# Tile 0's mean in two halves, tile 2 and tile 3 trade their way of transposing, and projections by quarters of the weights

## The chip, the cores and the metric

The kernel runs on one core of a Trainium2 chip. The metric is the device time of one launch in microseconds (us), the median of several runs. The core has five engines with instruction streams of their own that wait for each other by semaphores: TensorE (PE, matmuls; its weight loads are shown as PEld), VectorE (DVE), ScalarE (ACT), GpSimd (POOL) and SyncE (SP), which issues nearly all DMAs here. Matmuls write to PSUM, which has eight banks of 128 x 512 float32.

## The reference

A layer norm feeds a linear-attention block and a gated feed-forward block; the input and both results are added.

```python
x  = A_x                                   # 1 x 2048 x 512, bfloat16
xn = (x - mean(x)) / sqrt(var(x) + 1e-5)   # over the last axis

# A: linear attention, 32 heads of 16
q, k, v = split(xn @ wqkv)                 # wqkv 512 x 1536
phi = lambda t: where(t > 0, t + 1, exp(t)) + 1e-6
pq, pk = phi(q), phi(k)
kv  = einsum("bhsd,bhse->bhde", pk, v)
z   = einsum("bhsd->bhd", pk)
o   = (pq @ kv) / (pq . z + 1e-6)          # by head
A   = o @ wo                               # wo 512 x 512

# B: feed-forward, width 1792
B   = (silu(xn @ w_gate) * (xn @ w_up)) @ w_down

return x + A + B
```

## The kernel before, in words

The 2048 rows are 16 tiles of 128 rows (t = 0 to 15); a tile's 512 columns are four quarters of 128 (c = 0 to 3). There is no scheduler. The kernel calls small helpers in a hand-written order; each helper appends one operation to one engine's list through `K.op` or `K.dma` and names what it reads and writes, and a recording class (`_Prog`) works out the semaphore waits. An engine runs its list strictly in the order of the calls, so the order of the calls in the code is the order on each engine, and a waiting instruction holds back all that stands behind it on its engine.

The program has three stages.

1. *Start*, lines 593 to 700: tiles 0 to 4, written out by hand. This is where the change lies.
2. *Projection loop*, lines 706 to 735: for tiles 5 to 15, K = xn Wk and Q = xn Wq (`kproj`, `qproj`), the feature map of K, and `gtacc(t)`, which sums xn^T pk over the tiles in banks 4 to 7.
3. *FFN loop*, lines 978 to 1001: the gated feed-forward, the normalisation of Q and the output tiles.

What the start does for a tile, by helper:

- `xload` loads x, `wqkv_load` a part of Wq or Wk by quarters of its rows. They stand ahead of everything (lines 247 to 259). SP issues them one after the other; two go through ScalarE's queue.
- `bns` (bn_stats, line 296) and `agg` (bn_aggr, line 299) give mean and variance on VectorE, `eps` adds 1e-5 (VectorE or POOL), `rstd_of` raises to the power -0.5 on POOL (line 352).
- `mean_act(1)` (line 304) sums tile 1 on ScalarE with an accumulator, so that its mean needs no bn_stats.
- Tiles 0, 1 and 2 are not normalised ahead of their projections: they are only centred (`xc_half`, line 379, half a tile; `xc_full`, line 389, a whole one), and the scale rstd is applied when the projection is read out of PSUM (`first_ek`, `first_pk`, `first_pq`, lines 503 to 525).
- A centred tile is transposed either on TensorE, `tp_first` (two matmuls with the identity, line 407, and a copy to SBUF on ScalarE, line 416), or by a DMA on SP, `transpose_xc` (line 398). Before the change tiles 0 and 1 go through TensorE and tile 2 through the DMA.
- `proj_first(t, name, h)` (line 446) is half of a projection: two matmuls, quarters 2h and 2h+1.
- From tile 3 on, tiles are normalised whole (`xn_dve`, line 332), transposed by DMA into xnT (`transpose_dma`, line 423) and projected with `kproj` and `qproj` (line 432). ScalarE and VectorE make the features with `exp_k`, `exp_q`, `copy_q`, `clip_k` and `maxadd_k`.
- The FFN needs xnT of tiles 0 to 2 as well; their transposes run in the loop (lines 719 and 720), and `late_eq` makes their exponential of Q there (lines 727 and 728).
- `feat_pool(0)` makes tile 0's K feature on POOL, `first_feat` those of tiles 1 and 2 on VectorE. `xn_act(0)` normalises tile 0 on ScalarE, with `negmean(0)` on POOL for its bias.
- `fill(n, cols)` (line 268) issues matmuls on constants, whose result nobody reads, while TensorE has nothing else.

K of tile t uses bank 0 or 2 and Q bank 1 or 3 (even and odd t); the transposes of the start use banks 4 to 7.

## Time and profile before

| | |
|---|---|
| three timed runs | 210.83, 210.95, 211.18 us; median 210.95 |
| the profiled execution, its own time | 210.89 us |
| its span (first to last instruction) | 209.7 us |
| granted TensorE clock, mean | 1.00 |
| busy: TensorE, VectorE, POOL, ScalarE | 206.7, 119.4, 74.4, 70.2 us |
| VectorE busy, 0 to 5, 5 to 10, 10 to 15 us | 2.13, 4.29, 4.54 us |
| ScalarE busy, the same | 2.54, 4.64, 3.30 us |
| POOL busy, the same | 1.79, 3.19, 2.15 us |

Times inside the profile count from the start of the span. A row of the order of time reads: start, length, engine, line, operation, what it writes and reads, shape, how many were merged, and in brackets how long the engine had been idle before it and what ended that. A matmul of 512 columns is shown 0.38 us long, but matmuls overlap, so the next one starts much earlier: the distance of their starts is what they cost. Lists of waits read: who waited, for whom, us in total, how often, the longest.

DMA landings in the profile before, in us: x of tile 0 at 2.78, of tile 1 at 3.18, of tiles 2 to 5 at 5.92, 7.24, 8.42 and 8.74; Wk quarters 0 and 1 at 4.53, 3 at 4.67, 2 at 4.89; Wq quarters 0 to 3 at 6.27, 6.67, 7.67 and 8.09. The load of tiles 6 and 7 (256 KB) is issued at 8.60 and lands at 11.35.

### The profile page before, as it was taken

Reading aid. Unit: us, or ns where it says so; the run is one execution under the profiler, and the core shown is the slowest. Engines: PE = TensorE matmul, PEld = TensorE weight load, DVE = VectorE, ACT = ScalarE, POOL = GpSimd, SP = SyncE. Lnnn points to the kernel's source line nnn. Section 1 sums busy time; section 2 is a strip of 40 time slices with the busy share of each in tenths; the row PEclk is TensorE's granted clock in tenths of the full one; section 3 lists DMA queues with packets and bytes.
Section 4 is the critical chain, followed back from the end, with each engine's and each line's share of the span. In section 5 each row is a group of like instructions: output and inputs, shape, how many; then the busy total and the mean of one; then the engine's idle time right before and its main releaser. Section 6 shows DMA issues by size and latency. Waiting matters only on the chain.

```text
span 209.7 us, 2763 instructions
## 1 busy us (share of the span) xinstructions
PE 206.7 (99%) x983; PEld 94.7 (45%) x983; DVE 119.4 (57%) x243; ACT 70.2 (33%) x123; POOL 74.4 (35%) x96
## 2 busy tenths in 40 slices
PE   8999999999999999999999999999999999999996
PEld 3344444445444444444444444444444444444444
DVE  4899988336265774637355746365556535373222
ACT  5957667956633331302122312213031213121000
POOL 3648987567032443223141422240424132221200
DMA  6766344894791111010202110202021010410201
GB/s 204 196 182 172 69 88 100 276 363 138 218 347 34 22 28 26 27 25 28 50 2 50 25 28 25 50 0 50 4 49 25 27 25 25 49 30 27 50 25 53
DMA packets 30287, 16.84 MB, mean 80 GB/s; under 512 B 20928, under 2 KB 29632, under 8 KB 30272
## 3 DMA queue, kind: packets, MB, share of 16 engines
q1 hardware_dynamic: 29984, 16.39, 29.6%
q10 hardware_dynamic: 288, 0.26, 0.4%
q8 instruction: 8, 0.13, 0.3%
q14 instruction: 7, 0.06, 0.1%
HBM read 9.70 MB, written 2.10 MB: 56 GB/s over the span
## 4 chain that ended last, share of the span: by engine, by line
PE 95%; DMA 2%; SPq 2%; issue 0%; DVE 0%
PE psum L753 46%; PE psum L936 23%; PE psum L432 11%; PE psum L925 7%; PE psum L573 7%; DMA wqkv_sb<-in_A_wqkv_dram 2%; PE psum L446 1%; SPq L211 1%; SPq L204 1%; PE psum L851 0%; PE psum L874 0%; DVE out_sb L949 0%
## 5 line engine op out<-in xcount | busy, mean ns | idle before, releaser
L768 ACT ACTIVATE sg<-psum 128x512 bf16<-128x512 f32 x56 | 33.4, 598 | 106.8 <-PE psum L753 104.9
L753 PE MATMUL psum<-xnT,wg_sb 128*128 128x512 bf16 x224 | 57.5, 379 | 0.0
L753 PE MATMUL psum<-xnT,wu_sb 128*128 128x512 bf16 x224 | 57.5, 379 | 0.0
L883 POOL TENSOR_TENSOR prod<-pkq,zb 128x512 f32<-128x512 bf16 x16 | 18.6, 1161 | 57.7 <-DVE pkq L497 57.7
L753 PEld LDWEIGHTS psum<-xnT,wu_sb 128*128 128x128 bf16 x224 | 21.9, 98 | 26.4
L753 PEld LDWEIGHTS psum<-xnT,wg_sb 128*128 128x128 bf16 x224 | 21.9, 98 | 26.2
L949 DVE TENSOR_TENSOR out_sb<-psum,x_sb 128x512 bf16<-128x512 f32 (+2 forms) x17 | 11.2, 660 | 35.5 <-PE psum L936 35.5
L907 POOL TENSOR_TENSOR pqn<-pkq,rden 128x512 bf16<-128x512 bf16 x16 | 16.9, 1056 | 36.9 <-DVE rden L901 36.9
L774 DVE TENSOR_TENSOR pkq<-psum,sg 128x512 bf16<-128x512 f32 x28 | 19.1, 687 | 18.5 <-PE psum L753 14.0
L774 DVE TENSOR_TENSOR xn_sb<-psum,sg 128x512 bf16<-128x512 f32 x28 | 18.8, 673 | 14.9 <-PE psum L753 14.4
L936 PE MATMUL psum<-wd_sb,xn_sb 128*128 128x512 bf16 (+2 forms) x126 | 25.7, 355 | 0.0
L936 PE MATMUL psum<-wd_sb,pkq 128*128 128x512 bf16 x112 | 25.5, 379 | 0.0
L432 PE MATMUL psum<-wqkv_sb,xnT 128*128 128x512 bf16 x104 | 24.4, 379 | 0.0
L565 POOL TENSOR_TENSOR zacc<-zacc,pkq 128x512 f32<-128x512 f32 x15 | 17.3, 1156 | 5.0 <-DVE ek L488 4.6
L936 PEld LDWEIGHTS psum<-wd_sb,xn_sb 128*128 128x128 bf16 x126 | 11.8, 98 | 12.5
L936 PEld LDWEIGHTS psum<-wd_sb,pkq 128*128 128x128 bf16 x112 | 11.0, 98 | 13.2
L925 PE MATMUL psum<-m_sb,eq 128*128 128x512 bf16 (+2 forms) x68 | 16.6, 366 | 0.0
L573 PE MATMUL psum<-pkq,xn_sb 128*128 128x512 bf16 x64 | 16.1, 379 | 0.0
L432 PEld LDWEIGHTS psum<-wqkv_sb,xnT 128*128 128x128 bf16 x104 | 10.1, 98 | 12.3 <-ACT ek L505 0.3
L891 DVE TENSOR_REDUCE den<-prod 128x32 f32<-128x512 f32 x16 | 10.9, 684 | 5.4 <-POOL prod L883 5.3
L296 DVE BATCH_NORM_STATS2 stats<-x_sb 128x6 f32<-128x512 bf16 x16 | 10.9, 683 | 3.3 <-DMA x_sb<-in_A_x_dram 3.3
L497 DVE SCALAR_TENSOR_TENSOR pkq<-pkq,eq 128x512 bf16<-128x512 bf16 x16 | 11.1, 693 | 0.6
(65 smaller groups left out, 136.7 us busy)
## 6 DMA issues: line engine op xcount, KB each, us to landing
out_dram<-out_sb SPq DMA_DIRECT2D x15, 128.0 KB, 1.7
wg_sb<-in_B_w_gate_dram SPq DMA_DIRECT2D x2, 896.0 KB, 7.8
wu_sb<-in_B_w_up_dram SPq DMA_DIRECT2D x2, 896.0 KB, 6.1
wd_sb<-in_B_w_down_dram SPq DMA_DIRECT2D x1, 1792.0 KB, 9.8
x_sb<-in_A_x_dram SPq DMA_DIRECT2D x5, 256.0 KB, 3.0
x_sb<-in_A_x_dram SPq DMA_DIRECT2D x5, 128.0 KB, 3.3
wqkv_sb<-in_A_wqkv_dram SPq DMA_DIRECT2D x5, 128.0 KB, 3.5
wqkv_sb<-in_A_wqkv_dram SPq DMA_DIRECT2D x1, 512.0 KB, 7.8
```

Source lines behind the costliest of these rows:

```text
L432: (lambda c=c: pe.matmul(banks[b], xnT[:, c, t * P:(t + 1) * P], wqkv_sb[:, c, lo:lo + D], start=(c == 0), stop=(c == NDC - 1),))
L497: lambda: dve.scalar_tensor_tensor(out=dst, in0=src, scalar=0.0, in1=e, op0=ALU.max, op1=ALU.add,),
L565: lambda: pool.tensor_tensor(out=zacc[:, :], in0=zacc[:, :], in1=pk, op=ALU.add),
L573: (lambda c=c: pe.matmul(banks[4 + c], xn_sb[:, t, c * P:(c + 1) * P], pkq[:, t, 0, :], start=(t == 0), stop=(t == NT - 1),))
L753: (lambda c=c: pe.matmul(banks[b], w_sb[:, c, fc * P:(fc + 1) * P], xnT[:, c, C * 512:(C + 1) * 512], start=(c == 0), stop=(c == NDC - 1),))
L768: lambda: act.activation(sg[:, j % NSG, :], banks[gb], ACT.Silu),
L774: lambda: dve.tensor_tensor(out=hT(C, fc), in0=banks[ub], in1=sg[:, j % NSG, :], op=ALU.mult,),
L883: lambda: pool.tensor_tensor(out=p, in0=pkq[:, t, 1, :], in1=zb[:, :], op=ALU.mult),
L907: lambda: pool.tensor_tensor(out=pqn[:, t % NPN, :].rearrange("p (h e) -> p h e", e=DH), in0=pkq[:, t, 1, :].rearrange("p (h e) -> p h e", ...
L925: (lambda g=g: pe.matmul(dst, pqnT(t)[:, g, :], m_sb[:, g, lo:hi], start=(g == 0), stop=False,))
L936: (lambda fc=fc: pe.matmul(dst, hT(C, fc)[:, jj * P:(jj + 1) * P], wd_sb[:, fc, lo:hi], start=False, stop=(fc == NFC - 1),))
L949: lambda: dve.tensor_tensor(out=o, in0=src, in1=x_sb[:, t, lo:hi], op=ALU.add),
```

## The change

- *Tile 0's mean.* New `mean_parts(0)`: VectorE sums the first 256 columns with a tensor_tensor_reduce against ones (an instruction and a second one that reads the accumulator), ScalarE the other 256 with an accumulating copy. `xc_two` subtracts both partial means in one instruction of 256 columns. bn_stats of tile 0 runs after that, and its eps moves to VectorE. `negmean` and `xn_act` go; tile 0 is normalised by `xn_dve(0)` on VectorE, which waits for POOL's rstd of tile 0.
- *Fillers.* Seven instead of eight of 512 columns; the one of 128 columns goes.
- *Tile 2* is now transposed on TensorE (centred in halves, `tp_first(2, ...)` and the copy, now called `tc_first`).
- *Tile 3* is now centred, not normalised (`xc_full(3)`), transposed with `transpose_xc(3)` on SP, projected with `proj_first` and read out with `first_ek`, `first_pk`, `first_pq` and `first_feat`. Its xnT is made in the loop with those of tiles 0 to 2 (at t = 6), and `late_eq(3)` joins at t = 14.
- *Projections by quarters.* New `proj_part` is one matmul of a projection. K of tiles 0 and 1 is summed in the order of quarters 0, 1, 3, 2, with tile 1's transposes in between; Q of tiles 0 and 1 is begun with quarters 0 and 1, tile 2's transposes stand in between, and quarters 2 and 3 follow, tile by tile.
- *Order.* The load of tiles 6 and 7 moves from behind tile 2's DMA transpose to the end of the first loads; the later loads follow one place earlier. `gtacc(0)` stands behind the projections of tile 2, `gtacc(1)` and `gtacc(2)` behind those of tile 3. Buffers for three tiles become buffers for four (xc_sb, xcT), or are used in rotation (ek, kpos).

The diff, cut to its core:

```diff
-        xc_sb = sb("xc_sb", [3, D])
-        xcT = sb("xcT", [3 * NDC, P])
+        xc_sb = sb("xc_sb", [4, D])
+        xcT = sb("xcT", [4 * NDC, P])
...
         xload("sp", sp, 5, 1)
+        xload("sp", sp, 6, 2)
...
+        def mean_parts(t):
+            K.op(
+                "dve",
+                lambda: dve.tensor_tensor_reduce(
+                    out=scr2[:, :], in0=x_sb[:, t, 0:HD], in1=cx[:, 0:HD], scale=1.0 / D, scalar=0.0,
+                    op0=ALU.mult, op1=ALU.add, accum_out=mpart[:, 0:1],
+                ),
+                r=[("x", t)], w=[("mpa", t), ("scr2",)],
+            )
+            K.op(
+                "act",
+                lambda: act.activation(
+                    scr[:, 0:HD], x_sb[:, t, HD:D], ACT.Copy, scale=1.0 / D, accum_out=mpart[:, 1:2],
+                ),
+                r=[("x", t)], w=[("mpb", t), ("scr",)],
+            )
+
+        def xc_two(t, h):
+            K.op(
+                "dve",
+                lambda: dve.tensor_scalar(
+                    out=xc_sb[:, t, h * HD:(h + 1) * HD], in0=x_sb[:, t, h * HD:(h + 1) * HD],
+                    scalar1=mpart[:, 0:1], scalar2=mpart[:, 1:2], op0=ALU.subtract, op1=ALU.subtract,
+                ),
+                r=[("x", t), ("mpa", t), ("mpb", t)], w=[("xc", t, h)],
+            )
...
+        def proj_part(t, wname, c, pos):
+            lo, b = (D, kb(t)) if wname == "wk" else (0, qb(t))
+            K.op(
+                "pe",
+                lambda: pe.matmul(
+                    banks[b], xcT[:, NDC * t + c, :], wqkv_sb[:, c, lo:lo + D],
+                    start=(pos == 0), stop=(pos == NDC - 1),
+                ),
+                r=[("xcT", t, c // 2), (wname, c)], w=[bk(b)],
+            )
...
-        fill(8, 512)
-        stat(0)
-        negmean(0)
+        fill(7, 512)
+        mean_parts(0)
         mean_act(1)
-        xc_half(0, 0)
-        tp_first(0, 0, 4)
-        xc_half(0, 1)
-        tp_first(0, 1, 5)
-        fill(1, P)
+        xc_two(0, 0)
+        xc_two(0, 1)
+        bns(0)
         xc_half(1, 0, mact[:, 1, :], "mact")
         xc_half(1, 1, mact[:, 1, :], "mact")
+        agg(0)
+        eps(0, "dve")
+        tp_first(0, 0, 4)
+        tc_first(0, 0, 4)
+        tp_first(0, 1, 5)
+        tc_first(0, 1, 5)
         bns(1)
+        rstd_of(0)
+        xn_dve(0)
         agg(1)
         bns(2)
         agg(2)
+        xc_half(2, 0)
+        xc_half(2, 1)
+        bns(3)
+        agg(3)
+        proj_part(0, "wk", 0, 0)
+        proj_part(0, "wk", 1, 1)
+        tp_first(1, 0, 6)
+        tc_first(1, 0, 6)
+        tp_first(1, 1, 7)
+        tc_first(1, 1, 7)
+        proj_part(0, "wk", 3, 2)
+        proj_part(0, "wk", 2, 3)
+        first_ek(0)
+        clip_k(0)
+        xc_full(3)
+        bns(4)
+        eps(3, "dve")
+        proj_part(1, "wk", 0, 0)
+        proj_part(1, "wk", 1, 1)
+        proj_part(1, "wk", 3, 2)
+        proj_part(1, "wk", 2, 3)
+        proj_part(1, "wq", 0, 0)
+        proj_part(1, "wq", 1, 1)
+        transpose_xc(3)
+        xload("sp", sp, 8, 2)
+        proj_part(0, "wq", 0, 0)
+        proj_part(0, "wq", 1, 1)
+        first_pk(0)
+        tp_first(2, 0, 4)
+        tc_first(2, 0, 4)
+        tp_first(2, 1, 5)
+        tc_first(2, 1, 5)
+        agg(4)
+        bns(5)
+        proj_part(0, "wq", 2, 2)
+        proj_part(1, "wq", 2, 2)
+        proj_part(0, "wq", 3, 3)
+        first_pq(0)
+        eps(2, "pool")
+        rstd_of(2)
+        proj_part(1, "wq", 3, 3)
+        proj_first(2, "wk", 0)
+        proj_first(2, "wk", 1)
+        eps(1, "pool")
+        rstd_of(1)
+        first_ek(1)
+        clip_k(1)
+        first_pq(1)
+        xn_dve(1)
+        proj_first(2, "wq", 0)
+        proj_first(2, "wq", 1)
+        feat_pool(0)
+        gtacc(0)
...
+        proj_first(3, "wk", 0)
...
+        proj_first(3, "wq", 0)
+        proj_first(3, "wq", 1)
...
+        proj_first(3, "wk", 1)
+        first_ek(3)
...
+        gtacc(1)
+        gtacc(2)
+        xn_dve(3)
...
-            if t in (7, 8, 9):
-                transpose_dma(t - 7)
+            if t in (6, 7, 8, 9):
+                transpose_dma((3, 0, 1, 2)[t - 6])
...
-            if t in (11, 12, 13):
+            if t in (11, 12, 13, 14):
                 late_eq(t - 11)
```

More of the change, by code (lines that the diff above doesn't have):

```diff
@@ L156, in bass_parallel_sum__linear_attn_block__swiglu_ffn__prompt_kernel @@
         scr = sb("scr", [D])
+        scr2 = sb("scr2", [D // 2])
+        mpart = sb("mpart", [2], f32)
         pkq = sb("pkq", [NT, 2, D])
@@ L308, in mean_act @@
             )
-        def negmean(t):
-            K.op(
-                "pool",
-                lambda: pool.tensor_scalar(
-                    out=nb[:, t:t + 1], in0=mv[:, t, 0:1], scalar1=rstd[:, t:t + 1], scalar2=-1.0,
-                    op0=ALU.mult, op1=ALU.mult,
-                ),
-                r=[("mv", t), ("rstd", t)], w=[("nb", t)],
-            )
-        def xn_act(t):
-            K.op(
-                "act",
-                lambda: act.activation(
-                    xn_sb[:, t, :], x_sb[:, t, :], ACT.Identity, scale=rstd[:, t:t + 1], bias=nb[:, t:t + 1],
-                ),
-                r=[("x", t), ("nb", t), ("rstd", t)], w=[("xn", t)],
-            )
         def xn_dve(t):
@@ L413, in tp_first, with tc_first @@
             )
+        def tc_first(t, h, b):
+            tb = banks[b].bitcast(bf)[:, 0:HD].rearrange("p (c s) -> p c s", c=2)
             K.op(
@@ L504, in first_ek @@
             K.op(
-                "act", lambda: act.activation(ek[:, t, :], banks[kb(t)], ACT.Exp, scale=rstd[:, t:t + 1]),
-                r=[bk(kb(t)), ("rstd", t)], w=[("ek", t)],
+                "act", lambda: act.activation(ek[:, t % NE, :], banks[kb(t)], ACT.Exp, scale=rstd[:, t:t + 1]),
+                r=[bk(kb(t)), ("rstd", t)], w=[("ek", t % NE)],
             )
@@ L510, in first_pk @@
             K.op(
-                "act", lambda: act.activation(kpos[:, t, :], banks[kb(t)], ACT.Relu, scale=rstd[:, t:t + 1]),
-                r=[bk(kb(t)), ("rstd", t)], w=[("kpos", t)],
+                "act", lambda: act.activation(kpos[:, t % NE, :], banks[kb(t)], ACT.Relu, scale=rstd[:, t:t + 1]),
+                r=[bk(kb(t)), ("rstd", t)], w=[("kpos", t % NE)],
             )
@@ L529, in feat_pool @@
                 "pool",
-                lambda: pool.tensor_tensor(out=pkq[:, t, 0, :], in0=kpos[:, t, :], in1=ek[:, t, :], op=ALU.add),
-                r=[("kpos", t), ("ek", t)], w=[("pk", t)],
+                lambda: pool.tensor_tensor(out=pkq[:, t, 0, :], in0=kpos[:, t % NE, :], in1=ek[:, t % NE, :], op=ALU.add),
+                r=[("kpos", t % NE), ("ek", t % NE)], w=[("pk", t)],
             )
@@ L536, in first_feat @@
                 "dve",
-                lambda: dve.tensor_tensor(out=pkq[:, t, 0, :], in0=kpos[:, t, :], in1=ek[:, t, :], op=ALU.add),
-                r=[("kpos", t), ("ek", t)], w=[("pk", t)],
+                lambda: dve.tensor_tensor(out=pkq[:, t, 0, :], in0=kpos[:, t % NE, :], in1=ek[:, t % NE, :], op=ALU.add),
+                r=[("kpos", t % NE), ("ek", t % NE)], w=[("pk", t)],
             )
@@ L591, in xn @@
                 transpose_dma(t)
-        fill(8, 512)
-        stat(0)
-        negmean(0)
+        fill(7, 512)
+        mean_parts(0)
         mean_act(1)
-        xc_half(0, 0)
+        xc_two(0, 0)
+        xc_two(0, 1)
+        bns(0)
+        xc_half(1, 0, mact[:, 1, :], "mact")
+        xc_half(1, 1, mact[:, 1, :], "mact")
+        agg(0)
+        eps(0, "dve")
         tp_first(0, 0, 4)
-        xc_half(0, 1)
+        tc_first(0, 0, 4)
         tp_first(0, 1, 5)
-        fill(1, P)
-        xc_half(1, 0, mact[:, 1, :], "mact")
@@ L603, in bass_parallel_sum__linear_attn_block__swiglu_ffn__prompt_kernel @@
-        tp_first(1, 0, 6)
-        xc_half(1, 1, mact[:, 1, :], "mact")
-        tp_first(1, 1, 7)
-        proj_first(0, "wk", 0)
-        proj_first(0, "wk", 1)
-        first_ek(0)
+        tc_first(0, 1, 5)
         bns(1)
+        rstd_of(0)
+        xn_dve(0)
         agg(1)
-        eps(1, "pool")
         bns(2)
         agg(2)
-        xc_full(2)
-        proj_first(1, "wk", 0)
-        proj_first(1, "wk", 1)
-        first_pk(0)
+        xc_half(2, 0)
+        xc_half(2, 1)
+        bns(3)
@@ L618, in bass_parallel_sum__linear_attn_block__swiglu_ffn__prompt_kernel @@
+        proj_first(2, "wk", 0)
+        proj_first(2, "wk", 1)
+        eps(1, "pool")
         rstd_of(1)
         first_ek(1)
-        clip_k(0)
-        proj_first(0, "wq", 0)
-        feat_pool(0)
-        bns(3)
-        agg(3)
-        eps(3, "dve")
-        rstd_of(3)
-        proj_first(1, "wq", 0)
-        xn_act(0)
-        proj_first(0, "wq", 1)
-        first_pq(0)
-        bns(4)
-        agg(4)
-        eps(4, "pool")
-        proj_first(1, "wq", 1)
-        xn_dve(3)
         clip_k(1)
+        first_pq(1)
@@ L637, in bass_parallel_sum__linear_attn_block__swiglu_ffn__prompt_kernel @@
         xn_dve(1)
-        gtacc(0)
-        transpose_xc(2)
-        proj_first(2, "wk", 0)
-        proj_first(2, "wk", 1)
-        xload("sp", sp, 6, 2)
         proj_first(2, "wq", 0)
         proj_first(2, "wq", 1)
+        feat_pool(0)
+        gtacc(0)
+        eps(4, "pool")
+        rstd_of(4)
+        xn(4)
+        xload("sp", sp, 10, 2)
+        agg(5)
         first_pk(1)
         first_feat(1)
-        gtacc(1)
-        rstd_of(4)
-        xn_dve(4)
-        bns(5)
-        agg(5)
@@ L652, in bass_parallel_sum__linear_attn_block__swiglu_ffn__prompt_kernel @@
-        first_pq(1)
-        eps(2, "pool")
-        rstd_of(2)
+        proj_first(3, "wk", 0)
         first_ek(2)
@@ L657, in bass_parallel_sum__linear_attn_block__swiglu_ffn__prompt_kernel @@
         eps(5, "dve")
-        transpose_dma(3)
-        kproj(3)
-        qproj(3)
-        rstd_of(5)
-        transpose_dma(4)
-        xload("sp", sp, 8, 2)
         xn_dve(2)
+        proj_first(3, "wq", 0)
+        proj_first(3, "wq", 1)
         first_pk(2)
         first_feat(2)
-        gtacc(2)
-        xn_dve(5)
-        xload("sp", sp, 10, 2)
+        rstd_of(3)
+        rstd_of(5)
+        xn(5)
+        xload("sp", sp, 12, 2)
+        xload("sp", sp, 14, 2)
         bns(6)
-        exp_k(3)
+        first_pq(2)
+        proj_first(3, "wk", 1)
+        first_ek(3)
         clip_k(3)
+        zsum(0, 0)
+        first_pk(3)
         agg(6)
         eps(6, "pool")
-        rstd_of(6)
-        transpose_dma(5)
-        xload("sp", sp, 12, 2)
-        xload("sp", sp, 14, 2)
-        zsum(0, 0)
-        bns(7)
-        first_pq(2)
-        copy_q(3)
-        maxadd_k(3)
-        kproj(4)
-        xn(6)
-        exp_k(4)
-        qproj(4)
+        first_feat(3)
+        gtacc(1)
+        gtacc(2)
+        xn_dve(3)
+        bns(7)
+        kproj(4)
+        rstd_of(6)
+        xn_dve(6)
         agg(7)
         eps(7, "pool")
-        exp_q(3)
         rstd_of(7)
+        exp_k(4)
+        first_pq(3)
+        qproj(4)
+        stat(8)
         exp_q(4)
+        transpose_dma(6)
         copy_q(4)
         clip_k(4)
-        stat(8)
+        zsum(1, 1)
         xn(7)
-        zsum(1, 1)
         maxadd_k(4)
-        stat(9)
+        bns(9)
+        agg(9)
+        eps(9, "pool")
+        rstd_of(9)
         gtacc(3)
```

## The prediction

> **What bounds the kernel now.** I read first the chain that ended last, then TensorE's own waits, then the order of time engine by engine over the first 17 us.

> ```profile
> PE 95%; DMA 2%; SPq 2%; issue 0%; DVE 0%
> ```
> ```profile
> PE psum L268 <- PEq L1018: 0.8, 1, 0.8
> PE psum L446 <- DMA wqkv_sb<-in_A_wqkv_dram: 0.3, 1, 0.3
> ```
> ```profile
> 3.78 0.63 PE L268 MATMUL psum<-const-bfloat16-1.0 128*128 128x512 bf16 x1
> 4.21 0.62 PE L407 MATMUL psum<-ident,xc_sb 128*128 128x128 bf16 x4
> 4.63 0.25 PE L268 MATMUL psum<-const-bfloat16-1.0 128*128 128x128 bf16 x1
> 4.72 0.39 PE L407 MATMUL psum<-ident,xc_sb 128*128 128x128 bf16 x4
> 5.10 0.39 PE L446 MATMUL psum<-wqkv_sb,xcT 128*128 128x512 bf16 x1
> ...
> 7.27 0.59 PE L446 MATMUL psum<-wqkv_sb,xcT 128*128 128x512 bf16 x2
> 8.13 0.39 PE L446 MATMUL psum<-wqkv_sb,xcT 128*128 128x512 bf16 x1 [0.27 <-DMA wqkv_sb<-in_A_wqkv_dram]
> ```

> The chain is TensorE. Its second list has two waits: the start of the program, and once a weight load. Between 5.10 and the last matmul the starts of 512-column matmuls stand 0.216 us apart everywhere but at one place: from 7.49 (the second of the pair at 7.27) to 8.13 is 0.65, so 0.43 is lost to Wq (0.27 in brackets, since a matmul's modelled end lies 0.16 behind its successor's start). So the time is when the first weight matmul starts, plus a fixed amount of TensorE work, plus stalls. Only the first 12 us can change it.

> I compare at one point that both kernels reach with the same work done: the start of gtacc(3), when K and Q of tiles 0 to 4 and gtacc(0) to (2) are behind it. It is at 16.78 (L573). From 5.10 that is 52 matmuls of 0.216 (11.22), the 0.43, and 0.03 of small change.

> The start of that chain on VectorE and ScalarE:

> ```profile
> 2.80 0.69 DVE L296 BATCH_NORM_STATS2 stats<-x_sb 128x6 f32<-128x512 bf16 x1 [2.80 <-DMA x_sb<-in_A_x_dram]
> 3.53 0.18 DVE L299 BATCH_NORM_AGGREGATE mv<-stats 128x2 f32<-128x6 f32 x1
> 3.75 0.48 DVE L379 TENSOR_SCALAR xc_sb<-x_sb,mv 128x256 bf16<-128x256 bf16 x2
> ...
> 4.54 0.69 DVE L296 BATCH_NORM_STATS2 stats<-x_sb 128x6 f32<-128x512 bf16 x1
> ```
> ```profile
> 3.21 0.63 ACT L304 ACTIVATE scr<-x_sb 128x512 bf16<-128x512 bf16 x1 [0.91 <-DMA x_sb<-in_A_x_dram]
> 3.74 0.19 ACT L304 ACTIVATION_READ_ACCUMULATOR scr<-x_sb 128x1 f32 x1
> 4.66 1.21 ACT L416 ACTIVATE xcT<-psum 128x256 bf16<-128x256 bf16 x4 [0.74 <-PE psum L407]
> ```

> On VectorE an instruction that needs nothing new starts 0.09 before its predecessor's end (the two L379), and one that reads its predecessor's result 0.03 after it (3.49 to 3.53).

> **A: the first weight matmul, -0.41.** bn_stats and bn_aggr (2.80 to 3.71) leave the path for a half sum on each of two engines. [...] L949 takes 0.557 for 384 columns and 0.291 for 128, so 256 take 0.42. The read of its sum is not in this trace: nothing, to 0.18 (L299, another tiny result); I take 0.13, nearer the ScalarE read's 0.09 of extra time than nothing. Done at 3.35. The form itself is not in the trace either: 0.28 (L379, 256 columns) to 0.69 (L497, 512). *ScalarE half:* L304's 0.63 less 256 columns of 0.82 ns (from L481, 0.60 for 512, and L416, 0.39 for 256) is 0.42; its read ends 0.09 later; from 2.81, done at 3.32. The subtraction now has two per-partition operands: 0.284, plus 0.06 by L332 (0.41) against L389 (0.35). It runs 3.385 to 3.73. With one filler fewer TensorE is free at 3.78 (today the eighth holds it to 4.21), so the transposes of tile 0 start at 3.80. They are 0.11 apart and the second takes 0.31 to its end, 4.22; ScalarE copies 4.25 to 4.635 (L416), having finished tile 1's mean at 4.07. First weight matmul 4.69, behind its weights' landing at 4.53. Against 5.10: -0.41.

> **B: transposes behind that point, +0.44.** Today all eight stand ahead of 5.10. Now tile 1's four and four new ones of tile 2 stand behind 4.69. At 0.056 each (the last pairs at 4.72) 8 cost 0.44. The two copies of tile 2 fall into ScalarE's gap between first_pk(0), which ends at 7.4, and first_pq(0) at 8.86, and cost nothing; without that gap, 0.3 each.

> **C: the wait for Wq, -0.43.** By quarters, TensorE comes to Wq 0 at 6.73, 1 at 6.95, 2 at 8.02 and 3 at 8.45; they land at 6.27, 6.67, 7.67 and 8.09. Margins 0.46, 0.28, 0.35, 0.36. The 256 KB load of tiles 6 and 7 now issues at 6.0 instead of 8.60, but behind all of Wq on SP's queue, so I cost it at nothing.

> **D: new stalls, +0.53.** (1) Tile 1's K waits for its copy: transposes 5.12, copy 5.43 to 5.815, matmul at 5.87 where TensorE is free at 5.78: 0.09. (2) Tile 2's two pairs of transposes wait for VectorE: 0.12 and 0.09. (3) Tile 3 decides. VectorE's list, with the rows' durations: xc_two 3.385 and 3.645, bn_stats(0) 3.905, xc(1) 4.51 and 4.70, aggr(0) 4.90, eps(0) 5.115, bn_stats(1) 5.18 to 5.87. Then xn(0), newly on VectorE (0.41, ScalarE's 0.82 of L323 is gone), waits for POOL's rstd(0): 5.345 plus 0.62 (L352), so 6.01, and VectorE idles 0.23. Queued behind it are aggr(1) 6.34, bn_stats(2) 6.43, aggr(2) 7.155, xc(2) 7.375 and 7.575, bn_stats(3) 7.775, aggr(3) 8.50, clip(0) 8.595, xc(3) 8.795 to 9.15. SP issues the transpose at 9.175. Today's one landed 2.49 after its issue:

> ```profile
> 7.27 1.28 SPq L398 DMA_TRANSPOSE xcT<-xc_sb  x1
> ```

> So it lands at 11.665 and TensorE goes on at 11.70. Without this wait it would be there at 4.69 + 0.43 + 0.22 + 0.43 + 0.09 + 1.73 + 0.12 + 0.11 + 0.09 + 0.11 + 1.73 (Wq quarters 2, 3, then K of tile 2) + 0.86 (its Q) + 0.86 (gtacc(0)) = 11.47. Stall 0.23.

> Nothing else reaches the path. Tile 3's first_ek, first_pk, first_pq (0.69 each) and late_eq (0.64) replace three copies of 0.60: 0.9 more on ScalarE, which idles 0.69 an iteration at 29 us. feat_pool(0) now stands behind rstd(1) on POOL and ends at 10.45, 0.15 ahead of gtacc(0). SP carries 17 transposes as before; four instead of three in the back-to-back stretch from 24.6 can put the FFN weights 1.3 later, and they land at 41.7 for use at 47.2.

> **Sum:** -0.41 + 0.44 - 0.43 + 0.53 = +0.13, and the 0.03 that today's stretch holds is not there: **+0.10**. From 11.70 it is 24 matmuls, 5.18, to 16.88. The profiled execution took 210.89 (span 209.7 and 1.2 around it), 0.06 under the median of 210.95. Forecast **211.0**.

> Its ends: since stall (3) is set by VectorE's list, whatever is earlier or later there moves the end one for one, down to the other stalls. With the half sum and its read at 0.28 and nothing, ScalarE's 3.32 decides: -0.03. Without the second operand's price -0.12. At 0.69 and 0.18 it is +0.26; with the form at twice the 512-column row, 1.38, +0.95, which I think far off. The transpose's landing takes 2.4 at least, 2.5 in the middle, 4.0 at most (L423): -0.1 to +1.5.

> **Rivals.** *1, tile 3 in time:* if xc(3) is done 0.23 earlier, only 0.30 of stalls are left: -0.13, 210.76; with no stall at all -0.43, 210.46. For it: 0.23 is just VectorE's idle time at xn(0). Against: that list has no other slack. *2, the transpose comes late:* over 2.72 us from issue to landing it costs all it takes. At 14.03 and 16.59 it took 2.86 and 2.99, with 256 KB loads in flight, and the load of tiles 6 and 7 is in flight here. At 2.99: +0.60, 211.5. Against: at 9.74 and 11.19, with the same load in flight, 2.58 and 2.46. *3, the clock:* fillers run 0.427 apart until 4.6, then matmuls 0.216. TensorE had then worked for 3.8 us without a break. Now it stands idle from 4.23 to 4.69, 0.46, just when the step would come. If the count starts anew at 4.69, it comes at 8.50: half of 3.81 lost, 1.90, less the 0.53 of stalls that it swallows and the -0.41 + 0.44 - 0.43: 16.78 + 1.5, 212.4. It decides from the first idle time that counts as a break. Against: the break is an eighth of those 3.8 us, and today's profile has none to judge by.

> [...]

> **How the numbers follow.** This kernel's runs spread over 0.35 us (210.83 to 211.18), so 0.2%, 0.42 us, is about what a measurement can tell. Forecast 0.60, tile 3 in time 0.17, late transpose or a slower half sum 0.15, clock 0.08. Faster than 210.53 needs almost no stall left: half of rival 1, 0.08. Slower than 211.37: rivals 2 and 3 and a little of the forecast, 0.26. The rest, 0.66, is no change. The range runs from rival 1's best to rival 2 with a transpose of 3.3 us, 210.4 to 211.9; the clock's 212.4 is left out. The forecast's own is 210.7 to 211.35.

> **What would show it.** The first L473 matmul (the quarters' line) at 4.69, no DMA wait of Wq, then one stall of about 0.23 ahead of tile 3's K with the transpose as its cause, and gtacc(3) at 16.88. Tile 3 in time: no such stall, gtacc(3) by 16.65. The clock: matmuls 0.427 apart after 4.7. I am wrong altogether if TensorE waits behind 17 us.

## The result and the profile after

| | before | after |
|---|---|---|
| median of 13 runs of each | 210.96 us | 211.68 us |
| lowest and highest | 210.68, 211.57 | 211.44, 213.51 |
| the profiled execution, span | 209.7 | 211.7 |
| x of tile 0 landed | 2.78 | 3.21 |
| first weight matmul starts | 5.10 | 5.17 |
| gtacc(3) starts | 16.78 | 18.84 |
| from gtacc(3) to the end of the span | 192.87 | 192.87 |

The ratio of after to before is 1.0043, 95% interval 1.0023 to 1.0062: slower by 0.4%, where no change was forecast as the likeliest. The runs of after fall into two groups, ten from 211.44 to 211.94 and three from 212.95 to 213.51; the profiled execution is one of the three. The rows of gtacc(3), before and after:

```profile
16.78 1.03 PE L573 MATMUL psum<-pkq,xn_sb 128*128 128x512 bf16 x4
```
```profile
18.84 1.03 PE L598 MATMUL psum<-pkq,xn_sb 128*128 128x512 bf16 x4
```

The chain that ended last and TensorE's waits, of after:

```profile
PE 96%; DMA 2%; issue 1%; SPq 0%; DVE 0%
```
```profile
PE psum L271 <- PEq L1065: 0.8, 1, 0.8
PE psum L473 <- DMA wqkv_sb<-in_A_wqkv_dram: 0.3, 1, 0.3
PE psum L418 <- DVE xc_sb L378: 0.2, 1, 0.2
```

The chain is TensorE still. The wait for Wq is gone; the DMA in the second line is Wk now, quarter 0, which landed at 5.03 (4.53 before). No wait is left after that, so the 2.06 us at gtacc(3) are not waits. The order of time on TensorE shows what they are:

```profile
4.18 0.65 PE L418 MATMUL psum<-ident,xc_sb 128*128 128x128 bf16 x4 [0.19 <-DVE xc_sb L378]
5.17 1.01 PE L473 MATMUL psum<-wqkv_sb,xcT 128*128 128x512 bf16 x2 [0.34 <-DMA wqkv_sb<-in_A_wqkv_dram]
5.97 0.63 PE L418 MATMUL psum<-ident,xc_sb 128*128 128x128 bf16 x4
6.40 3.74 PE L473 MATMUL psum<-wqkv_sb,xcT 128*128 128x512 bf16 x10
9.98 0.39 PE L418 MATMUL psum<-ident,xc_sb 128*128 128x128 bf16 x4
10.20 1.03 PE L473 MATMUL psum<-wqkv_sb,xcT 128*128 128x512 bf16 x4
```

Ten matmuls of 512 columns take the 3.58 us from 6.40 to 9.98, and four after 10.20 take 0.87 to the next group: up to about 9.3 they start 0.427 apart, half rate, behind that 0.216. The busy time of engines by stretches of the span tells the same (stretch; its length; busy us and instructions of PE, PEld, DVE, ACT, POOL; granted clock; DMA share; GB/s), first after, then before:

```profile
4.60:9.30 4.70, 4.36 (x15) 1.73 (x14) 4.49 (x17) 2.58 (x6) 1.99 (x5) 1.00 0.87 270
```
```profile
4.60:9.30 4.70, 4.43 (x26) 1.96 (x24) 3.99 (x13) 4.28 (x9) 2.98 (x6) 1.00 0.81 233
```

TensorE is as busy in both and does 15 instructions instead of 26. The granted clock is 1.00 in both: that column does not show this step, only the distance of the starts does.

The new instructions themselves cost what was forecast. VectorE's start:

```profile
3.23 0.42 DVE L361 CUSTOM_DVE_ANT_0 scr<-x_sb,const-bfloat16-1.0 128x256 bf16<-128x256 bf16 x1 [3.23 <-DMA x_sb<-in_A_x_dram]
3.58 0.08 DVE L361 DVE_READ_ACCUMULATOR2_ANT mpart<- 128x1 f32 x1
3.78 0.60 DVE L378 TENSOR_SCALAR xc_sb<-x_sb,mpart 128x256 bf16<-128x256 bf16 x2
```

The half sum is 0.42 (forecast 0.42), its read ends 0.01 behind it (forecast 0.13), and xc_two is 0.345 each (forecast 0.344). ScalarE's half and its read, done at 3.74, end last of the two; the prediction had VectorE's last, by 0.03. From the landing of x to the first transpose it is 0.97 us, against 1.43 before. But x landed 0.43 later.

### The profile page after: what moved, and what is told of

It reads as the page before. It is cut to its first block, busy times and chain, and to the rows that moved or that the text cites. A ratio compares the mean times of both kernels' runs of the same rounds, so it can differ in the third digit from the quotient of the medians.

```text
span 211.7 us, 2759 instructions
## 1 busy us (share of the span) xinstructions
PE 207.6 (98%) x967; PEld 95.2 (45%) x985; DVE 120.1 (57%) x249; ACT 71.5 (34%) x127; POOL 73.7 (35%) x94
## 2 busy tenths in 40 slices
DMA packets 30287, 16.84 MB, mean 80 GB/s; under 512 B 20928, under 2 KB 29632, under 8 KB 30272
## 4 chain that ended last, share of the span: by engine, by line
PE 96%; DMA 2%; issue 1%; SPq 0%; DVE 0%
PE psum L800 45%; PE psum L983 23%; PE psum L446 10%; PE psum L972 7%; PE psum L598 6%; PE psum L473 3%; DMA wqkv_sb<-in_A_wqkv_dram 2%; PE psum L460 2%; PE psum L898 0%; PE psum L921 0%; PE psum L418 0%; SPq L206 0%; DVE out_sb L996 0%
## 5 line engine op out<-in xcount | busy, mean ns | idle before, releaser
L800 PE MATMUL psum<-xnT,wu_sb 128*128 128x512 bf16 x215 | 56.7, 379 | 0.5
L446 PE MATMUL psum<-wqkv_sb,xnT 128*128 128x512 bf16 x94 | 22.3, 379 | 0.1
L446 PEld LDWEIGHTS psum<-wqkv_sb,xnT 128*128 128x128 bf16 x96 | 9.4, 98 | 11.3 <-issue 0.3
L336 POOL TENSOR_TENSOR rstd<-vpe,nhalf 128x1 f32<-128x1 f32 x16 | 9.4, 591 | 7.7 <-DVE vpe L327 6.6
```

Source lines behind the costliest of these rows:

```text
L446: (lambda c=c: pe.matmul(banks[b], xnT[:, c, t * P:(t + 1) * P], wqkv_sb[:, c, lo:lo + D], start=(c == 0), stop=(c == NDC - 1),))
L800: (lambda c=c: pe.matmul(banks[b], w_sb[:, c, fc * P:(fc + 1) * P], xnT[:, c, C * 512:(C + 1) * 512], start=(c == 0), stop=(c == NDC - 1),))
```

## The experiments

Four theories were tried. Their letters, in the expectations, are their own and not the prediction's terms. *Theory A*, which the expectations call the clock, is that idle time of TensorE ahead of the first weight matmul puts the step to full rate off. *Theory C* is a collision on VectorE and GpSimd behind 15 us, where the change puts a sum of GpSimd (`zsum`) beside tile 3's features. *Theory D* is the landing of tile 0's x, which differs between executions (2.78 to 3.31 us in twelve traces): before, the wait for Wq swallows a late x; after the change nothing does. *Theory B*, in the first expectations, is rival 2 of the prediction, a late transpose of tile 3. A text that sets another theory beside these says what it is.

The rows that the readings below rest on, from the trace of one execution of each kernel (us). "Forecast with its x" is the prediction's 16.88 for gtacc(3), moved by as much as x landed behind 2.78. The step to full rate is where the distance of matmul starts halves, for 512 columns from 0.427 us (half rate) to 0.216 (full rate):

| kernel | x 0 landed | first weight matmul | step to full rate | gtacc(3) | forecast with its x | that execution |
|---|---|---|---|---|---|---|
| before | 2.78 | 5.10 | 4.7 | 16.78 | | 210.89 |
| after | 3.21 | 5.17 | 9.3 | 18.84 | 17.31 | 212.95 |
| again1 (after) | 3.30 | 5.15 | by 5.1 | 17.32 | 17.40 | 211.96 |
| zsum_moved | 3.20 | 5.04 | 6.0 | 17.28 | 17.30 | 211.76 |
| fill_gap | 3.31 | 5.18 | 4.9 | 17.33 | 17.41 | 212.62 |
| fill_both | 2.81 | 5.27 | 5.3 | 17.06 | 16.91 | 212.05 |
| zsum_fill | 3.27 | 5.21 | 6.6 | 17.55 | 17.37 | 211.66 |
| zsum_fill8 | 3.11 | 5.10 | 4.7 | 17.14 | 17.21 | 213.19 |

**The changed kernel once more** (again1), unaltered.

> The changed kernel once more, unaltered, for a second trace. Its profiled execution of before (212.95 us) ran matmuls 0.427 us apart until about 9.3 us. Theory A (the clock: TensorE's new idle stretches ahead of the first weight matmul let the step to full rate come later, at a moment that differs from execution to execution): the step to 0.216 comes later than 4.7 here too, and the start of gtacc(3) is late against 16.8 by half the time between the first weight matmul and the step, less the stalls that this swallows. Theory B (the late transpose of tile 3): the step comes near 4.7, and TensorE waits ahead of tile 3's K by 0.5 us or more, with the transpose's landing over 11.9.

It took 211.96, beside 211.03 for the kernel before. The step came before 5.15, so the half rate of the first profile is not in every execution. Yet gtacc(3) started at 17.32. Theory B does not explain it: tile 3's transpose took 2.50 us from issue to landing, and TensorE waited 0.29 for it, not 0.5 or more:

```profile
10.99 1.03 PE L598 MATMUL psum<-pkq,xn_sb 128*128 128x512 bf16 x4
12.14 1.89 PE L460 MATMUL psum<-wqkv_sb,xcT 128*128 128x512 bf16 x7
```

Four matmuls from 10.99 leave TensorE free at 11.85; the transpose landed at 12.01. (Eight matmuls follow; one record is missing, as happens in these traces.) Then gtacc(4) waited, behind the point where the prediction had looked. TensorE's wait, and VectorE and GpSimd ahead of it:

```profile
PE psum L598 <- DVE pkq L522: 0.3, 1, 0.3
```
```profile
15.36 0.28 DVE L513 TENSOR_SCALAR ek<-ek 128x512 bf16<-128x512 bf16 x1
15.55 0.17 DVE L302 BATCH_NORM_AGGREGATE mv<-stats 128x2 f32<-128x6 f32 x1
15.74 1.12 DVE L562 TENSOR_TENSOR pkq<-kpos,ek 128x512 bf16<-128x512 f32 x1
16.78 0.40 DVE L316 TENSOR_SCALAR xn_sb<-x_sb,mv,rstd 128x512 bf16<-128x512 bf16 x1
```
```profile
15.70 0.61 POOL L586 CAST zacc<-pkq 128x512 f32<-128x512 bf16 x1 [1.31 <-DVE ek L513]
16.29 0.65 POOL L327 TENSOR_SCALAR vpe<-mv 128x1 f32<-128x1 f32 x1
17.02 0.58 POOL L336 TENSOR_TENSOR rstd<-vpe,nhalf 128x1 f32<-128x1 f32 x1
```

first_feat(3) (L562) takes 1.12 instead of 0.69 where zsum's CAST runs beside it, and eps (L327, one column) 0.65 instead of 0.22 beside first_feat. All that VectorE does for tile 4 is late by that, and gtacc(4) starts 0.42 late (0.26 in that wait's own count, 0.16 of it the modelled overlap of matmuls).

L562 reads kpos and ek, began 0.04 behind the CAST of 0.61, and took 0.43 longer; eps took 0.43 longer beside L562. That the two pairs collide is read from these times; by what means, the trace does not show.

**Theory C by itself** (zsum_moved): the sum over tile 0 goes behind the wait, everything else stays.

```diff
-        zsum(0, 0)
         first_pk(3)
...
+        zsum(0, 1)
         zsum(1, 1)
```

> The changed kernel with POOL's first sum of K features, zsum(0), moved from beside tile 3's feature add on VectorE to the place ahead of zsum(1). Theory C (that add took 1.12 us instead of 0.69 in the second trace, started within 0.04 of POOL's zsum(0), and TensorE waited 0.42 for tile 4's K feature at 19.7): the add takes 0.69, the 0.42 at gtacc(4) is gone or under 0.15, median 211.2 to 211.4, ratio to the kernel before 1.001 to 1.002. Theory A (clock alone): 211.6 to 211.8, ratio 1.003 to 1.004, as the changed kernel.

Measured 211.51 (12 runs, 211.27 to 213.28; ratio to before 1.0028, 1.0008 to 1.0047). VectorE at the same place:

```profile
15.45 0.18 DVE L302 BATCH_NORM_AGGREGATE mv<-stats 128x2 f32<-128x6 f32 x1
15.64 0.69 DVE L562 TENSOR_TENSOR pkq<-kpos,ek 128x512 bf16<-128x512 f32 x1
16.25 0.41 DVE L316 TENSOR_SCALAR xn_sb<-x_sb,mv,rstd 128x512 bf16<-128x512 bf16 x1
```

L562 is 0.69 again and the wait at gtacc(4) is gone. The median is 0.17 lower than that of after, and 0.37 over the kernel before of its own batch, against 0.72; its interval overlaps after's, so the size of theory C is not settled; that L562 takes 1.12 beside the CAST and 0.69 without it is shown. Part of the gain is lost again in this trace: TensorE waits 0.17 at 20.91 and 0.20 at 23.70 for the transposes of tiles 6 and 7. Two of the twelve runs were at 212.89 and 213.28: the late group has another cause.

**Theory A: TensorE's idle time filled** (fill_gap: six fillers of 128 columns behind tile 0's transposes; fill_both: the eighth wide filler besides, the first two lines of the diff).

```diff
-        fill(7, 512)
+        fill(8, 512)
...
         tp_first(0, 1, 5)
+        fill(6, P)
```

> The changed kernel with six filler matmuls of 128 columns between tile 0's transposes and its first weight matmul, so that the idle stretch there is filled, and nothing else altered. Theory A: fewer executions with a late step, median 210.9 to 211.3 and ratio to the kernel before 1.000 to 1.0015, none or few over 212.5. Theory B: the fillers change nothing, 211.5 to 211.9, ratio 1.003 to 1.005.

> As fill_gap, and with the eighth 512-column filler of the kernel before put back, so that TensorE has no idle stretch from its first filler to its first weight matmul even where x of tile 0 lands late. Price of the eighth filler: it holds tile 0's transposes to 4.2, so the first weight matmul comes near 5.1 instead of 4.7 if x lands early, up to 0.3 us. Theory A: no execution over 212, median 210.9 to 211.3. Theory B: 211.6 to 212.2, as the late transpose stays and the eighth filler's price may come on top.

Both are slower than after, not faster: 212.80 (6 runs; ratio to before 1.0084, 1.0069 to 1.0098) and 212.35 (1.0058, 1.0045 to 1.0072). The step came at 4.9 and 5.3, and gtacc(3) was in its place. What they lost came later: TensorE waited 0.73 and 0.52 us at 21 us for tile 6's transpose, which took 3.74 and 3.53 us instead of 2.71 (again1). What went with that is shown with the last run below. The wait at gtacc(4) is in both too, 0.42 and 0.33.

**Theory A in the kernel before** (before_gap): four wide fillers less, so TensorE idles 1.8 us ahead of its transposes.

```diff
-        fill(8, 512)
+        fill(4, 512)
```

> The kernel before with four instead of eight 512-column fillers, nothing else altered: TensorE idles from about 2.6 to 4.1 us. Theory A: the step to full rate comes late in most executions; median 211.5 to 212.7, with a wide spread, although tile 0's transposes can start 0.1 us earlier. Theory B: the fillers do nothing for the time, 210.8 to 211.0, ratio 0.999 to 1.000.

212.10 (6 runs; ratio 1.0052, 1.0033 to 1.0072). The step came at 7.9 instead of 4.7 (matmuls start 0.427 apart up to 7.80 and 0.216 from 8.07 on), and gtacc(3) at 17.79, 1.0 later. So with 1.8 us of idle time ahead of the first weight matmul the step is put off, by 3.2 us here.

With at most 0.25 us of idle time ahead of the first weight matmul the step came at 4.7 (before, zsum_fill8), 5.1 (before_quarters) and 5.3 (fill_both). The 7.9 of before_gap lies 2.6 us behind the last of these. The runs of the kernel before show no such late step: it would cost about 1 us, as in before_gap, and its 15 runs beside before_halves lie within 0.92 us (210.75 to 211.67).

What a shorter gap does is not settled. With 0.6 to 1.0 us of idle time, in two to four pieces, the step came by 4.1 (halves_quarters, below; 0.3 of it idle by then), at 4.9 (fill_gap), by 5.1 (again1), at 5.2 (before_halves), 6.0 (zsum_moved), 6.6 (zsum_fill) and 9.3 (after), in no order of the idle time; after and again1 are the same kernel and idled 1.0 us each. The same filler of 128 columns in halves_quarters, at full rate, and in before_halves, at half rate:

```profile
4.46 0.22 PE L270 MATMUL psum<-const-bfloat16-1.0 128*128 128x128 bf16 x1
```
```profile
4.66 0.31 PE L270 MATMUL psum<-const-bfloat16-1.0 128*128 128x128 bf16 x1
```

So theory A is shown for a gap of 1.8 us. For the changed kernel the traces show only that the step is late in some executions, and not what decides in which.

**Theory D: x of tile 0 behind the first weights** (before_xlate, after_xlate).

```diff
+        wqkv_load("sp", sp, "wk", 1, 0, 2)
+        xload("act", act, 1, 1)
         xload("sp", sp, 0, 1)
-        xload("act", act, 1, 1)
-        wqkv_load("sp", sp, "wk", 1, 0, 2)
```

> The kernel before with the load of tile 0's x issued behind the first load of Wk instead of ahead of it, so that x lands some 0.45 us later; nothing else altered. Theory D (x of tile 0 landed anywhere from 2.78 to 3.31 in the six traces; in the kernel before the wait for Wq, 0.43, swallows a late x, in the changed kernel nothing does): 0 to 0.15 us over the kernel before, ratio 1.000 to 1.001, and the wait for Wq shrinks to under 0.1. Against it (a late x costs both kernels alike): plus 0.4 to 0.5, ratio 1.002.

> The changed kernel with the same swap of the two loads. Theory D: the whole delay comes through, 0.35 to 0.5 us over the changed kernel, 212.0 to 212.2, ratio to the kernel before 1.005 to 1.006. Against it: the same small price as in the kernel before, 211.7 to 211.8.

213.80 and 214.23. Both expectations missed: the exchange delayed x by 1.9 and 1.5 us (it landed at 4.69 and 4.75), not by some tenths, TensorE idled 1.8 and 1.9 us ahead of its transposes, and the step came at 10.1 and 9.3. So much delay brings theory A into both kernels. It decides nothing on theory D.

**The quarters alone** (before_quarters): the prediction's term C in the kernel before.

```diff
-        proj_first(0, "wq", 1)
+        proj_part(0, "wq", 2, 2)
+        proj_part(1, "wq", 2, 2)
+        proj_part(0, "wq", 3, 3)
...
-        proj_first(1, "wq", 1)
+        proj_part(1, "wq", 3, 3)
```

> The kernel before with one part of the change alone: quarters 2 and 3 of Q 0 and Q 1 summed quarter by quarter (2, 2, 3, 3). The prediction credited the end of the wait for Wq with 0.43. Theory D: that wait was cover; with it gone TensorE waits for POOL's K feature of tile 0 and for tile 2's transpose instead, which stand 0.25 and 0.3 behind, and the time is within 0.15 us of the kernel before, ratio 0.9993 to 1.0005. Prediction's reading: minus 0.3 to 0.43, ratio 0.998 to 0.9986.

211.03 (11 runs; ratio 0.9995, 0.9984 to 1.0006): no change. In its trace x landed at 3.08, the first weight matmul came at 5.27, 0.17 later than in before's, and waits of 0.19 (for Wq's quarter 2, which landed at 8.01), 0.06 (for xn(0) on ScalarE, at gtacc(0)) and 0.09 (for tile 3's transpose) stand where 0.43 was. By itself the term is worth nothing that can be measured.

**The half sum alone** (before_halves) **and with the quarters** (halves_quarters). In both, tile 0's bn_stats goes behind tile 1's centring, since the half sum takes its place:

```diff
-        fill(8, 512)
-        stat(0)
-        negmean(0)
+        fill(7, 512)
+        mean_parts(0)
         mean_act(1)
-        xc_half(0, 0)
+        xc_two(0, 0)
...
         tp_first(1, 1, 7)
+        stat(0)
+        negmean(0)
```

> Before with the change's first part alone: tile 0's mean in two halves on VectorE and ScalarE, xc_two, 7 instead of 8 wide fillers; bns(0), agg(0), eps and rstd of tile 0 go behind tile 1's centring. All else is before's, so Q 0 and Q 1 still wait for Wq's quarters as halves. Theory D (the wait for Wq, 0.43 us in before, swallows whatever lies ahead of it): the first weight matmul comes some 0.4 earlier relative to x 0's landing, the wait for Wq grows by as much, and the time is before's, 210.9 to 211.1. If the prediction's term A counts by itself: 210.5 to 210.6. If TensorE's idle time ahead of the first weight matmul (theory A) matters in the middle execution: 211.5 and above with the step to full rate behind 7 us.

> The same with Q 0 and Q 1 summed by the weights' quarters (2, 2, 3, 3) besides: the prediction's terms A and C together, without B (the transposes among the weight matmuls) and without D (tile 2 and tile 3 trading their way). If A and C add up as the prediction has them, 210.2 to 210.5. If Wq's last quarter itself sets when the Q matmuls end (in the kernel with quarters alone small waits of 0.19, 0.06 and 0.09 took the place of the 0.43), 210.8 to 211.1: then no part of the change could gain, and its credit C was the term at fault. Theory A: an idle TensorE puts the step to full rate off in some executions, up to 212.5.

211.69 and 211.70 (6 runs each; ratios 1.0030, 1.0018 to 1.0041, and 1.0029, 1.0018 to 1.0041): slower. Theory A had such a figure for before_halves, but with a step behind 7 us, and the step came at 5.2 and by 4.1. TensorE in halves_quarters, the last Q matmuls and gtacc(0):

```profile
7.75 1.03 PE L488 MATMUL psum<-wqkv_sb,xcT 128*128 128x512 bf16 x4
9.67 0.60 PE L613 MATMUL psum<-pkq,xn_sb 128*128 128x512 bf16 x2 [0.90 <-ACT xn_sb L325]
```

The fourth matmul of the first row starts at 8.40, so TensorE is free for gtacc(0) at 8.61, although x had landed at 3.11; in before it was 9.01, with x at 2.78. So the two terms, with the earlier step, do pay 0.40 up to here. Then it waits 1.06. bn_stats(0), at 2.80 in before, now starts at 4.82; rstd(0), first_ek(0), feat_pool(0) and xn(0) all hang on it, and xn(0) ends at 9.62, feat_pool(0) at 9.28. before_halves loses the same way (0.74). What the half sum takes off the path to the first weight matmul it puts on the path to gtacc(0), and the changed kernel can only have the gain because it also moves gtacc(0) behind tile 2's projections.

**One and two fillers without the collision** (zsum_fill: zsum_moved and a wide filler behind tile 0's transposes; zsum_fill8: the eighth wide filler ahead of them besides, the first two lines of the diff).

```diff
-        fill(7, 512)
+        fill(8, 512)
...
         tp_first(0, 1, 5)
+        fill(1, 512)
         tc_first(0, 1, 5)
```

> The changed kernel with zsum(0, 1) late, as in the kernel with that alone (211.51), and one wide filler (0.43 us) behind tile 0's second transpose, where TensorE stood idle between 4.6 and 5.2 us. Theory A: no execution near 213 is left, the middle stays at 211.4 to 211.5. If TensorE's 16 KB of instructions (queue q8) come some 0.4 us earlier by the filler and lie on another transpose, 211.6 to 211.9 with a wait for xnT behind 20 us. If the filler delays tile 1's transposes: the first weight matmul later by up to 0.2 and the time 211.7.

> The kernel of zsum_fill with an eighth wide filler ahead of tile 0's transposes (as before has), so that TensorE's idle time from 3.78 to the transposes at 4.24 is filled too. In the profile of zsum_fill the step to full rate came at 6.4 us, behind the first two weight matmuls and tile 1's four transposes, which took 0.40, 0.43 and four times 0.107 in place of 0.216 and 0.056: some 0.6 us in all. Theory A in its wider form (each idle stretch ahead of the first weight matmul puts the step off by some tenths in most executions, not by 4 us in a few alone): the step comes at 4.7 to 5.3 and the middle of the times falls to 210.9 to 211.2. Theory D (x 0 lands late and nothing absorbs it): nothing changes, 211.5 to 211.7. If x 0 lands early, at 2.8, the filler itself holds the transposes up by up to 0.4, and the middle stays too.

zsum_fill: 211.59 (9 runs, 211.37 to 211.66; ratio 1.0023, 1.0012 to 1.0033). No run near 213 is left, of nine; with two or three in a dozen in zsum_moved and after, that is what theory A expects but could be chance in one case of seven or so (0.8 to the ninth power is 0.13). zsum_fill8: 213.23 (4 runs, 212.82 to 213.50; ratio 1.0097, 1.0075 to 1.0118), 1.5 us and more above what either theory had. The step came at 4.7 and gtacc(3) at 17.14, 0.36 behind before with an x 0.33 later. Then TensorE:

```profile
19.73 1.03 PE L598 MATMUL psum<-pkq,xn_sb 128*128 128x512 bf16 x4
22.52 0.82 PE L446 MATMUL psum<-wqkv_sb,xnT 128*128 128x512 bf16 x3 [1.76 <-DMA xnT<-xn_sb]
```

and the DMA view of that execution, in the stretch from 19.0 to 21.0 (queue and kind: packets, MB, share of 16 engines), and of the transposes issued at 17.54 and 19.09 (count, median us from issue to landing):

```profile
q8 instruction: 1, 0.02, 5.0%
```
```profile
xnT<-xn_sb SPq DMA_TRANSPOSE x1, 4.9
```
```profile
xnT<-xn_sb SPq DMA_TRANSPOSE x1, 4.7
```

One packet of 16 KB of instructions is fetched at 19.39 and is under way for 1.6 us; the two transposes in flight take 4.9 and 4.7 us. That queue q8 carries TensorE's instructions is read from its distances: in before its eight fetches come 211 to 277 of TensorE's matmuls and weight loads apart, while the counts of the other engines differ far more (VectorE 26 to 53, ScalarE 8 to 45, GpSimd 7 to 34). The same is seen in twelve of the fourteen traces: a fetch starts 1.0 to 2.4 us behind a transpose's issue, and the transpose takes 3.5 to 4.9. Eight of the fourteen:

| kernel | fetch starts | the transpose it meets, issue to landing | for tile | needed |
|---|---|---|---|---|
| before | 20.12 | 18.25 to 22.29, 4.04 | 7 | later: hidden |
| again1 | 21.63 | 19.70 to 23.76, 4.06 | 7 | later: hidden |
| zsum_fill | 21.04 | 19.15 to 23.34, 4.20 | 7 | later: hidden |
| zsum_moved | 21.52 | 19.18 to 23.57, 4.39 | 7 | TensorE waits 0.20 |
| fill_gap | 19.30 | 18.17 to 21.91, 3.74 | 6 | TensorE waits 0.73 |
| fill_both | 18.79 | 17.81 to 21.34, 3.53 | 6 | TensorE waits 0.52 |
| zsum_fill8 | 19.39 | 17.54 to 22.48, 4.93 | 6 | TensorE waits 1.93 |
| halves_quarters | 23.10 | 20.92 to 23.38, 2.46 | 8 | at its end: no loss |

The five others that agree took 4.0 to 4.1, on tile 7's transpose (after, before_quarters, before_halves and the two with exchanged loads). In before_gap the fetch starts 0.68 behind an issue, at 26.26, and that transpose took 3.19. The 130 transposes issued in the first 30 us with no such fetch in their flight took 2.4 to 3.4. No run moves a fetch and nothing else, so that the fetch is the cause is read from these coincidences. In the changed kernel, with seven or eight fillers the fetch lies on tile 7's transpose, which has room or nearly; with nine and more it comes earlier (18.79 to 19.39 in three traces) and lies on tile 6's. By this reading that is what fill_gap and fill_both lost behind 18 us: in their traces the step came by 5.3, but the fetch had moved. Without its wait zsum_fill8's execution would be at 213.19 - 1.93 = 211.26, which is worked out, not run. No kernel here beats the one before.

## Why the prediction was right or wrong

*The measure held.* All rests on gtacc(3) and a fixed remainder: 192.87 us of span behind it in before, in after and in zsum_fill alike, and more only where a trace shows waits behind it.

*A, -0.41: right in size, wrong in where it starts.* From x's landing to the first transpose 0.97 instead of 1.43 is -0.46; forecast were 1.02 and -0.41. For VectorE's half the forecast took the new form to run as fast as L949, an addition; the trace of before does not show that form, and in after it took 0.42 for 256 columns. But the first weight matmul came at 5.04 to 5.27, not 4.69, above all because x of tile 0 did not land at 2.78. In the twelve traces without an exchange of loads it landed at 2.78 to 3.31, in the middle at 3.16; before's profile happened to be the earliest of all. Wk's quarter 0, which the prediction has at 4.53, spreads as well: it landed at 4.51 to 5.08 in the seven traces of the change, and in after TensorE waited for it, so that an early x would not always have given 4.69.

*B, +0.44: right.* Eight transposes at full rate are 0.056 apart (the rows at 5.54 and 8.03 in zsum_fill8's trace).

*C, -0.43: this is the step that failed.* The wait for Wq is gone in every trace of the change, as forecast. But it was no free 0.43: TensorE waited there until Wq landed, however early or late its work had begun. By the rows of before an x up to some 0.3 later than 2.78 costs nothing there: 0.13 of it is lost in the eighth filler (in before_quarters x was 0.30 later and the first weight matmul 0.17), and gtacc(0), at 9.01, has 0.19 of room behind xn(0), which ended at 8.72 (in before_quarters gtacc(0) started 0.10 behind xn(0)'s end). In after a late x costs all it is late. The prediction compared a landing of 2.78 on both sides, and took the whole wait as a gain over a median that paid next to nothing for late landings. With x in the middle, 3.16, its 16.88 becomes 17.26 and before's 16.78 some 16.84: +0.10 becomes some +0.4.

The table's forecast with its x is within 0.2 us of gtacc(3) in all six traces of the change with the step by 7 us. Only in again1, fill_gap and zsum_fill8 is that the sum's own terms; in fill_both the six small fillers hold the first weight matmul back to 5.27, in zsum_moved and zsum_fill the step comes at 6.0 and 6.6, and fewer stalls of D make up for it. That x lands late and that the change pays for it is shown by these traces; that the kernel before swallows it rests on the sum and on before_quarters (gtacc(3) 0.06 later): a kernel with x delayed by a few tenths and nothing else was not run.

*D, +0.53: right in size.* (1) was 0.10 in again1 (forecast 0.09), (2) 0.10 instead of 0.21, and (3), ahead of tile 3's projection, 0.29 (forecast 0.23), with a transpose of 2.50 us as forecast. In zsum_fill8's trace (3) looks like 0.47, with ScalarE as its cause, but one matmul is missing there: eight weight loads stand beside seven matmuls.

```profile
11.93 1.42 PEld L460 LDWEIGHTS psum<-wqkv_sb,xcT 128*128 128x128 bf16 x8 [0.56 <-ACT kpos L536]
```
```profile
12.18 1.67 PE L460 MATMUL psum<-wqkv_sb,xcT 128*128 128x512 bf16 x7 [0.31 <-ACT ek L530]
```

The first load starts 0.10 behind the transpose's landing at 11.83, as in again1 (12.01 and 12.12; the prediction let TensorE go on 0.04 behind a landing), so (3) was some 0.25 there. Where the step came late, (2) and (3) were gone (zsum_fill, after), as rival 3 said.

*"Nothing else reaches the path", and nothing behind 17 us: wrong.* again1 waited 0.42 at gtacc(4). The prediction followed tile 3 as far as its transpose and counted the rest of VectorE's and GpSimd's lists as unchanged; it did not see that zsum(0) and first_feat(3) fall together.

*Rival 3, the clock: right in price, too low in chance.* It had gtacc(3) at 16.78 + 1.5, which is 18.71 with after's x; measured were 18.84, with the step 4.1 us behind the first weight matmul (forecast 3.81). It had 0.08; of the changed kernel's 13 runs three show that time. Its mechanism, a count that starts anew behind the break, is not shown: again1 had the same idle time and no late step. Nor is it shown that the step is the clock's: the granted clock reads 1.00 on both sides of it. The late step makes the tail, not the median: where the step comes at 6.0 to 6.6, the stalls of D swallow most of it.

*The forecast of no change* thus missed by 0.7 us in the median: some 0.4 for x in the middle on both sides, the rest from the collision on GpSimd and a late step in part of the executions. How these two share that rest was not measured apart. That the time lies inside the stated range is luck: its upper bound was drawn for a late transpose, which did not come.

## What to carry to other kernels

A wait that is visible in one profile may absorb the spread of something ahead of it; before it is booked as a gain, ask how late each input can land, from several traces, and what will absorb it when the wait is gone. A sum made at one point of equal work has to be followed by a look along all engines' lists behind that point. And fillers are not free: here the fetch read as TensorE's instructions moved with their number, and a transpose that TensorE needed took 3.53 to 4.93 us beside it, against 2.71 in again1. Last, a gap of 0.22 us in a list of matmuls can be a missing record: the weight loads beside it tell.
